# A new stored order, and a new split between VectorE and ScalarE, for a fused attention and MoE kernel

## The chip, the cores and the metric

The kernel runs on one core of a Trainium2 chip. The time is that of the device, in microseconds (us): three runs of the kernel before gave 565.9, 566.43 and 566.93, median 566.43. The profile is of one execution, and its span, from the first to the last instruction, is 563.2 us.

## The reference

Two stages. The first is a linear attention with a complex decay, for 4 batches and 8 heads of 768 positions and 48 dimensions. The second is a feed-forward layer over the 3072 rows that the first one leaves.

```python
scale = np.minimum(mag, 0.999) / (mag + 1e-06)      # mag = |a|
for t in range(S):
    S_re, S_im = ar * S_re - ai * S_im + k[t] v[t]^T, ar * S_im + ai * S_re
    y[:, :, t] = q[:, :, t] @ S_re
h = x @ w_in                                        # x: 3072 x 384, w_in: 384 x 2048
out = (h * sigmoid(1.702 * h)) @ w_out              # w_out: 2048 x 384
```

## The kernel before

The 768 positions of a batch are three units of 256, so there are 12 units (u = 0 to 11), each of two chunks of 128. A unit goes through three stages.

*prepare* turns the decay into running products (scans over time) and multiplies them into q and k. Unit 0 does it in two parts of 128 positions, so that its first chunk can start early. The lines that count here: L393, L409 and L427 are scans, L401 and L402 a reciprocal of 3 columns, L437 and L440 belong to the angle, and L271 is the product (`qr` and `qk` are q and k with the factors in). POOL copies three columns (L458), then SP issues five DMAs for each of the two tensors (L469 to L472) that spread the heads over the partitions of `qkh`.

*attend* works on `qkh` with small matmuls on quarters of the array. A group is one entry of the plan: P (L507, scores into `p_ps`, 32 profiled matmuls), T (L563, two transposes of k into `kz_ps`), X (L532, output into `x_ps`, 8 to 32 matmuls) and Z (L557, the new state into `kz_ps`, 32 matmuls). Between them VectorE masks the scores (L511, `pm`), and ScalarE or VectorE copies the transposes (L566 or L567, `kt`) and the result (L542 or L543).

*moe* is the feed-forward layer, in blocks of one unit (blocks 0 and 1) or two units (blocks 2 to 6). Blocks 0 and 1 use float32 weights `valA` and `valU`. The later ones split every number into two fp32r halves and take three matmuls for a product, of 128x512. L613 is the first product (into `h_ps`) and L646 the second (into `o_ps`). Between them come the activation (L626, ScalarE), the high half (`gh`, a cast: L629 on ScalarE or L630 on VectorE) and the low half (`gl`, L632, VectorE).

The weights arrive as 64-bit words in four buffers `raw`. ScalarE takes one half (L294), VectorE the other (L291, then a shift L295), and L298 adds them into `valA` or `valU`. A buffer can be loaded again when its sum is done. Later the float32 weights are split in two (L307 or L308, and L310). In the rest of the run, 58 looks at the inputs (`raw_w`, L675 to L699) test whether this fast path holds.

The order of all this is not found at run time. Each of the 1,827 operations is an entry of a plan, with an engine, a function and the entries it depends on. A table `ORDER` holds the sequence in which they are written into the program, and that fixes the sequence on each engine; an engine takes its own instructions in that sequence and waits at each for what it needs. The set `OTHER` lists those of 282 entries with two forms, one for ScalarE and one for VectorE, that take the second form. When an entry needs a ScalarE function table other than the current one, a table load (L843) is put ahead of it.

Before the first attention there are 13 entries (L454, 26 profiled matmuls) that only keep TensorE busy until real work is there; the result is not used.

Of the kernel before, what the change touches and what calls it, by code (L numbers as in the profile page):

```python
# [106 lines left out]
}  # L107
ORDER = (
    "08jve0000A00jUK0A&DD08s!_0D}O808{{l0962n09F8p09OEr09gP509XKB0E++v0Eqw#09pWF09yc$00sbz0FVG&0A2u!0AT=)0AK)-0Am1-"
    "0Ac|U0FwZ}00#hQ0I2|y0G9w{0BHaM0BQgX0A~PZ0Bitj0F(f20Ga^^0B!*Z0F?l50SW+{0B``70C50w0TBS40GR-u0CE8m0G$930CWJK0D%CQ"  # L110
    "0H6R30CfQq0CoVP0Tcjt0HFY*0C)fr01*JB0HpyH00aQC0T}?Q0Hy&J0H*+X0Sf@L0JH!I0D1uz0H^?~0JQ)K0T=+b0IUHT022Uv0IdMH0DJ)-"
    "02u&%03!f?0Ji}k01g1I02BbP0J#8v0k#1f0Vn{v03HCq0J{O00I&eO0KovU0Vx2z0Kx#i0LTEt0K@>v0UZFv0V)8-0UiMi0UQ7%0LlQz0Du7@"
    "03`s_0VM#-0NMa10V4q`0U`hz0M!5|0M-B-02Kf?0N?-|02Tox0N4QB0k{Cy0L%a#0W1K{0NDT+0k;4x03QI)0O9}`0NVf{03iS<0WJX00Ve?A"
    "0MP+003rb105|~S05SmG0l5I*0VV;u0WbjP0lNV&0WkpN0lxvf0WtvQ0W$%;0L=lw05bsX04V{!04@M30PFxO05t&80W<*a0ObHI0W|>V0Sy5*"
    "051SK0O|ng05AYK0mA_605JgX05k!`0P+FB05$<Q0mcEs0S*B306YQ20Mh}-06_po0Pq3M0m%Um0YL#d0YU*o0Pz7j0Ym}M0XG4r0Y?Bk0XqQo"
    "0X+f8080Tp0Yw4J0QdpQ0Z0M<0Zjo(0Qmqt0Y(5m0nh<H0ZIWs06zfq0Qvy?06+mw0iXd(073!M0agG<0QLb_0Z#x!07L;$07wB$07U^<0YCuv"
    "0a*Y^0hRzv0RI8e07?K&0Z{<{0RaF`0n`D^0n-5d0nGvc0o4Hg0sjHk0RRC~0s#S20oMW80a^f00aOA40ipq10s{d80bK!A0t5mG0bT)O0ha;>"
    "0onoy0cipU0oeiD0b>FV0o(y!0uKRb0tEqO0v7=T0crvY0dE2f0;U050b~LV0t*5d0uTXo0R#aB0c!zn0R{pR0ucff0uuq>0bl{>0rUaj0cHW-"
    "0vQ1Z0cQcS0viEg0qFv#0ki>Z0jdFU0vZCX0pS650;mD%0pbC50vrOV0v!St0c`<r0;&Ps0dfKB0hs}$0eS+f0v`dI0u=#s0w4mg0v-YG0qg>?"
    "0;~cd0rdgz0ek`D0ptR-0p$Vk0rmlV0h|Hx0wV!<0eu3p0qp`L0<{7n0p<aQ0<!^k0h<Ay0wn?R0jvVJ0rvu~0f7OX0=fZt0p|j*0rLT{0fzyf"  # L120
    "0=5Bw0=WYF0=EJ90e%7|0j>hS0=xl(0x$w60r>*J0x<#l0=ohG0x|+T0sH}f0fGX-0{j7l0sR8Q0w@AA0{sDn0>lFX0jL5g0f_;K0yF|D0yY9G"
    "0yhFZ0{#Ll0xbcd0yqLL0gVFx0zLvY0yzRd0xtoh0y+Xl0?z{g0g3{?0y_f*0=)r?0|o-e0gM7i0zd(e0>}c!0!RWu0|5fb0geJf0!acx0>T1H"
    "0z?8#0>uH40!0E#0|NsG0#gFZ0i^>30|^3B0#^dc0}2BO0?Y#q0?h(V0g(d_0!{&v0$l=F0}cZV0#pJ|0#ySH0h0rm0$c)F0h9t(0$~Fb0$KwR"
    "0$u@?0jC2M0?-2x0#E|k0$Ty80$&3b0%ihY0$>7B0?q<t0%!vh0~i8h1DXR80%rpm0@?!61DOLC0~-Qm0&4@C0~!My0%-%B0^0&?0&xQ!0^9>0"
    "0jmOP1DyhG0@MQ110VyU0^I?v0^b861ET_N0^kFr0^S3j1Em6R1EvDg1E&KY0&fGV0&)W)0(AqR0j~n#1FQn(1D^ub0^$PJ0&@c60_6hN0`CK%"
    "0(%1R1E>Pn1E~V>1FiwF0(t^=10(|E0(1iB0(b)Q0(=5@1F-`20_XyL1F{110_g(k0)GLs0_y_y0_*{`10@1}273bc1FHgs1MCAP0{8>70__5M"
    "27Cjw0`vp011AE20{H_d11<uD27LoB27Uti1FZsr0)YeV1Fr+M0)qqY0)_*(27dyF0*M1K0*(TT12G1G1GWN)27v?f13Cha1Gxf=1G)l?27&^U"
# [890 lines left out]
```

## Time and profile before

| | |
|---|---|
| median of 3 runs | 566.43 us (565.9 to 566.93) |
| span of the profiled execution | 563.2 us |
| TensorE (PE) busy | 532.4 us, 95% |
| VectorE (DVE) busy | 447.3 us, 79% |
| ScalarE (ACT) busy | 313.2 us, 56% |
| first matmul | at 24.61 us |
| first matmul of the feed-forward layer | at 43.63 us |
| first matmul of block 2 (128x512) | at 154.22 us |
| last matmul | at 558.94 us |

The profile gives busy time by engine, in total and for any stretch, what every engine waited for, and the instructions in order of time. The own time of the profiled execution is not listed; its span is 3.2 us under the median of the runs, so about that much lies around the span. A busy TensorE is not one at its peak: matmuls overlap, so the distance from start to start counts, not the duration. For a 128x512 matmul in a row of its kind this distance is 0.227 us, while the row shows 0.39.

### The profile page before, as it was taken

How to read it: one execution, taken by the hardware profiler on the slowest of the kernel's cores; microseconds unless marked ns; L12 is line 12 of the kernel's file. 1: busy time of each engine (PE TensorE's matmuls, PEld its weight loads, DVE VectorE, ACT ScalarE, POOL GpSimd, SP SyncE). 2: the span in 40 equal slices, each digit the busy share in tenths (PEclk: the TensorE clock that was granted, in tenths of full speed). 3: DMA queues.
4: the chain of work that ended last, by engine and by line, in shares of the span. 5: the costliest groups of instructions: out<-in, count | busy, mean ns of one | idle time of the engine just before them, and what ended most of it. 6: DMA issues, size and time to landing. Idle time of an engine off the chain costs nothing.

```text
span 563.2 us, 14767 instructions
## 1 busy us (share of the span) xinstructions
PE 532.4 (95%) x6236; PEld 442.2 (79%) x6236; DVE 447.3 (79%) x820; ACT 313.2 (56%) x460; POOL 24.5 (4%) x86
## 2 busy tenths in 40 slices
PE   0289999999999999999999999999999999999997
PEld 0268888888888888888888888888888888888885
...
GB/s 307 199 194 359 181 381 76 222 102 221 72 146 119 128 148 101 113 150 122 136 180 75 167 128 210 45 227 94 103 138 56 203 122 87 51 52 70 29 61 110
DMA packets 30902, 80.06 MB, mean 142 GB/s; under 512 B 4208, under 2 KB 7024, under 8 KB 30832
## 3 DMA queue, kind: packets, MB, share of 16 engines
...
q14 instruction: 21, 0.17, 0.1%
HBM read 55.44 MB, written 4.72 MB: 107 GB/s over the span
## 4 chain that ended last, share of the span: by engine, by line
PE 92%; DVE 5%; ACT 1%; DMA 1%; issue 0%; DVEq 0%
PE o_ps L646 37%; PE h_ps L613 37%; PE x_ps L532 7%; PE p_ps L507 5%; PE kz_ps L563 4%; PE kz_ps L557 3%; DVE s L427 1%; DVE qk L271 1%; DMA ri<-in_a_dram 1%; DVE pm L511 1%; DVE s L271 0%; DVE qr L271 0%; DVE s L409 0%; DVE s L393 0%; DVE valA L298 0%
## 5 line engine op out<-in xcount | busy, mean ns | idle before, releaser
L626 ACT ACTIVATE g<-h_ps 128x512 f32<-128x512 f32 x80 | 46.3, 596 | 120.8 <-PE h_ps L613 79.7
L613 PE MATMUL h_ps<-xhi,hiA 128*128 128x512 f32 x240 | 95.9, 400 | 0.0
L646 PE MATMUL o_ps<-gh,hiU 128*128 128x512 f32 x240 | 95.5, 398 | 0.0
L646 PE MATMUL o_ps<-gl,hiU 128*128 128x512 f32 x240 | 93.7, 390 | 0.0
L613 PE MATMUL h_ps<-xhi,loA 128*128 128x512 f32 x240 | 93.6, 390 | 0.0
L646 PE MATMUL o_ps<-gh,loU 128*128 128x512 f32 x240 | 93.5, 390 | 0.0
L613 PE MATMUL h_ps<-xlo,hiA 128*128 128x512 f32 x240 | 93.5, 389 | 0.0
L843 ACT ACT_TABLE_LOAD x61 | 78.3, 1283 | 1.9 <-PEq L1006 0.8
L630 DVE CAST gh<-g 128x512 fp32r<-128x512 f32 x70 | 29.4, 421 | 42.5 <-PE o_ps L646 25.5
L632 DVE TENSOR_TENSOR gl<-g,gh 128x512 fp32r<-128x512 f32 x80 | 54.5, 684 | 3.0 <-ACT gh L629 1.3
L646 PEld LDWEIGHTS o_ps<-gl,hiU 128*128 128x128 f32 x240 | 45.0, 188 | 10.0 <-DVE gl L632 0.4
L613 PEld LDWEIGHTS h_ps<-xhi,loA 128*128 128x128 f32 x240 | 45.0, 188 | 9.6
L680 DVE TENSOR_REDUCE fit<-raw_w 128x1 f32<-128x256 f32 x96 | 38.1, 413 | 18.0 <-DMA raw_w<-in_w_out_dram 17.7
L646 PEld LDWEIGHTS o_ps<-gh,hiU 128*128 128x128 f32 x240 | 45.1, 188 | 9.2 <-issue 0.4
L646 PEld LDWEIGHTS o_ps<-gh,loU 128*128 128x128 f32 x240 | 45.1, 188 | 8.7
L613 PEld LDWEIGHTS h_ps<-xlo,hiA 128*128 128x128 f32 x240 | 45.1, 188 | 8.5
L613 PEld LDWEIGHTS h_ps<-xhi,hiA 128*128 128x128 f32 x240 | 45.1, 188 | 8.5
L511 DVE TENSOR_TENSOR pm<-p_ps,mask 128x512 f32<-128x512 f32 x48 | 32.8, 682 | 17.2 <-PE p_ps L507 13.9
L566 ACT ACTIVATE kt<-kz_ps 128x224 f32<-128x224 f32 x66 | 23.3, 353 | 40.5 <-PE kz_ps L563 29.9
L271 DVE TENSOR_TENSOR qk<-qk,s 128x768 f32<-128x768 f32 (+1 forms) x52 | 45.7, 889 | 0.0
L646 PE MATMUL o_ps<-g,valU 128*128 128x256 f32 x192 | 45.3, 380 | 0.0
L613 PE MATMUL h_ps<-x,valA 128*128 128x256 f32 x192 | 45.0, 381 | 0.0
...
## 6 DMA issues: line engine op xcount, KB each, us to landing
...
```

Source lines behind the costliest of these rows:

```text
L271: add(en, t, rank, lambda: e.tensor_tensor(out=out, in0=a, in1=b, op=alu), **kw)
L507: mm(p_ps[to : to + QL, j, lo:L], lhsT=at(h, 1, c)[:, lo : lo + QL], rhs=at(h, 0, c)[:, lo:L], start=True, stop=True)
L511: add("DVE", d_t(CW), rk(4 * c + hh), lambda hh=hh: dve.tensor_tensor(out=pm[hh], in0=p_ps, in1=mask, op=ALU.mult), r=["P"], w=[f"pm{hh}"])
L532: mm(x_ps[32 * j : 32 * j + 32, r, :], lhsT=lt, rhs=rt, start=n == 0, stop=n == len(steps) - 1)
L566: one = ("ACT", a_t(2 * KD) - 0.12, lambda e=e: act(out=kt[0][:, 2 * e : 2 * e + 2, :], in_=k_ps, func=AF.Copy))
L613: mm(h_ps[hb][:, hs], lhsT=ww[:, r * T + f * P : r * T + (f + 1) * P], rhs=x[:, r, :], start=r + k == 0, stop=r == NR - 1 and k == len(ter ...
L626: add("ACT", a_t(N) - 0.15, rk(i + f / 2), lambda hb=hb, hs=hs: act(out=g32[hb][:, hs], in_=h_ps[hb][:, hs], func=AF.Silu, scale=SLOPE), r ...
L630: two = ("DVE", d_t(N, 2), lambda hb=hb, hs=hs: dve.tensor_copy(out=high.g(hb)[:, hs], in_=g32[hb][:, hs]))
L632: add("DVE", d_t(N), rk(i + f / 2), lambda hb=hb, hs=hs: dve.tensor_tensor(out=glo[hb][:, hs], in0=g32[hb][:, hs], in1=high.g(hb)[:, hs].b ...
L646: mm(o_ps[m][:, 0:N], lhsT=y[:, f * DM + m * P : f * DM + (m + 1) * P], rhs=x[:, hs], start=i == 0 and f == 0 and k == 0, stop=i == NP - 1 ...
L680: add("DVE", d_t(CK), rk + 2, lambda x=x, op=op: dve.tensor_reduce(out=f_w[:, x, n : n + 1], in_=weights.looked_at()[:, :, 1], op=op, axis ...
L843: nc.scalar.preload_act_table_set(o[5])
```

## The change

Two tables are replaced: `ORDER`, the sequence, and `OTHER`, the entries in their second form. No operation is added or taken away, and the functions are the same. (Two more lines in `OTHER` move every line number behind it by 2, so L613 of before is L615 of after.)

```diff
 OTHER = {
-    260, 261, 262, 349, 351, 412, 418, 420, 426, 432, 434, 436, 440, 449, 489, 491, 497, 511, 512, 522,
...
+    262, 341, 402, 403, 404, 424, 426, 428, 440, 449, 511, 512, 580, 597, 600, 607, 610, 620, 630, 637,
...
 ORDER = (
-    "08jve0000A00jUK0A&DD08s!_0D}O808{{l0962n09F8p09OEr09gP509XKB0E++v0Eqw#09pWF09yc$00sbz0FVG&0A2u!0AT=)0AK)-0Am1-"
...
+    "08jve0000F0A&D|00jWQ0I2{`015z70E7Tj08{{j0962m09gQ50EPeo09pWD0EYkr0A2uF0Ehrr09*hN0E+-&0EqyK0FMA;0E_@)0FVHY0F3}-09"
...
```

`OTHER` grows from 51 entries to 113. Entries for VectorE fall from 718 to 662, and those for ScalarE rise from 399 to 455. The largest part is the cast `gh`: 38 more of them are ScalarE's and 5 more VectorE's. Table loads rise from 61 to 66.

On VectorE, in the head of the program, this stood behind the second part of unit 0 and around its last products (`qr`, `qk`), up to the first mask of scores (`raw_71` to `raw_74` are the four weight buffers):

```order
L291 TENSOR_SCALAR valA_238<-raw_74 128x768
L271 TENSOR_TENSOR qk<-qk,s_84 128x3x128
L295 TENSOR_SCALAR raw_73<-raw_73 128x768
L271 TENSOR_TENSOR s_82<-s_82,s_81 128x3x256
L271 TENSOR_TENSOR qr<-qk,s_80 128x3x128 x2
L295 TENSOR_SCALAR raw_74<-raw_74 128x768
L271 TENSOR_TENSOR qk<-qk,s_85 128x3x128
L298 ISA valA_154<-raw_71,valA_154 128x1536
L271 TENSOR_TENSOR qk<-qk,s_85 128x3x128
L370 SCALAR_TENSOR_TENSOR s_81<-ri,s_82 128x3x256
L295 TENSOR_SCALAR raw_72<-raw_72 128x768
L511 TENSOR_TENSOR pm_95<-p_ps,mask 128x512
```

The two shifts among the products (L295 of `raw_73` and `raw_74`) now stand behind them. In the same place there is now:

```order
L293 TENSOR_SCALAR valU_229<-raw_73 128x768
L293 TENSOR_SCALAR valA_233<-raw_72 128x768
L273 TENSOR_TENSOR qk<-qk,s_83 128x3x128
L442 TENSOR_SCALAR small<-s_85 128x3
L300 ISA valA_154<-raw_71,valA_154 128x1536
L273 TENSOR_TENSOR s_82<-s_82,s_81 128x3x256
L273 TENSOR_TENSOR qk<-qk,s_84 128x3x128
L273 TENSOR_TENSOR qr<-qk,s_80 128x3x128 x2
L273 TENSOR_TENSOR qk<-qk,s_85 128x3x128 x2
L372 SCALAR_TENSOR_TENSOR s_81<-ri,s_82 128x3x256
L513 TENSOR_TENSOR pm_95<-p_ps,mask 128x512
```

The shifts L297 (L295 of before) of `raw_74` and `raw_73` come between this mask and the next one.

On TensorE, a typical short burst of attention between feed-forward matmuls (here within block 3) was P followed by T:

```order
L613 MATMUL h_ps_106<-xhi_2082,loA_1187 128x512
L507 MATMUL p_ps<-qkh_76 32x128 x4
L507 MATMUL p_ps<-qkh_76 32x96 x4
L507 MATMUL p_ps<-qkh_76 32x64 x4
L507 MATMUL p_ps<-qkh_76 32x32 x4
L563 MATMUL kz_ps<-ident,qkh_76 128x112 x2
L646 MATMUL o_ps_107<-gh_1749,hiU_1196 128x512
```

In the order of after it is T that comes first (again within block 3):

```order
L615 MATMUL h_ps_106<-xhi_2174,loA_1272 128x512
L565 MATMUL kz_ps<-ident,qkh_76 128x112 x2
L509 MATMUL p_ps<-qkh_76 32x128 x4
L509 MATMUL p_ps<-qkh_76 32x96 x4
L509 MATMUL p_ps<-qkh_76 32x64 x4
L509 MATMUL p_ps<-qkh_76 32x32 x4
L648 MATMUL o_ps_107<-gh_1765,hiU_747 128x512
```

From the first feed-forward matmul on there were 64 such bursts, 33 of them begun by T and 56 ended by T. There are now 66, of which 63 begin with T and 29 end with it.

## Rows read from the trace of the kernel before

**Rows 1.** What PE waited for: total us, times, longest; the largest.
```profile
PE h_ps L454 <- DVE small L440: 24.6, 1, 24.6
```

**Rows 2.** Busy time by stretch: stretch, length, then PE, PEld, DVE, ACT, POOL.
```profile
24.60:43.60 19.00, 17.00 (x326) 12.99 (x326) 18.68 (x30) 15.19 (x24) 2.30 (x6) 1.00 0.61 193
43.60:154.20 110.60, 110.60 (x1509) 95.02 (x1509) 106.56 (x175) 93.62 (x140) 6.51 (x20) 1.00 0.67 199
```

**Rows 3.** PE in order of time, first feed-forward group: start, us, operation.
```profile
43.63 5.43 PE L613 MATMUL h_ps<-x,valA 128*128 128x256 f32 x24
```

**Rows 4.** PE in order of time, the last two matmuls.
```profile
558.94 0.19 PE L716 MATMUL p_ps<-small 128*1 128x1 f32 x2
```

**Rows 5.** DVE in order of time, within 24 to 42 us.
```profile
24.50 0.55 DVE L291 TENSOR_SCALAR valA<-raw 128x768 int32<-128x768 int32 x1
24.97 0.55 DVE L271 TENSOR_TENSOR qk<-qk,s 128x384 f32<-128x384 f32 x1
25.44 0.55 DVE L295 TENSOR_SCALAR raw<-raw 128x768 int32<-128x768 int32 x1
25.91 0.95 DVE L271 TENSOR_TENSOR s<-s,s 128x768 f32<-128x768 f32 x1
...
28.78 0.95 DVE L298 CUSTOM_DVE_ANT_0 valA<-raw,valA 128x1536 uint16<-128x1536 uint16 x1
29.64 0.55 DVE L271 TENSOR_TENSOR qk<-qk,s 128x384 f32<-128x384 f32 x1
...
30.98 1.01 DVE L295 TENSOR_SCALAR raw<-raw 128x768 int32<-128x768 int32 x1
...
40.74 0.69 DVE L511 TENSOR_TENSOR pm<-p_ps,mask 128x512 f32<-128x512 f32 x1 [0.25 <-PE p_ps L507]
41.35 0.68 DVE L383 TENSOR_SCALAR s<-s 128x768 f32<-128x768 f32 x1
41.95 0.94 DVE L437 SCALAR_TENSOR_TENSOR s<-s,s 128x768 f32<-128x768 f32 x1
```

**Rows 6.** Line L401: count, duration ns shortest/median/longest, first and last start.
```profile
L401 DVE TENSOR_SCALAR small<-s x13: 143/160/1140, 13.1 to 421.1; 128x3 f32<-128x3 f32 x13
```

**Rows 7.** POOL in order of time, two stretches of the head.
```profile
13.22 0.98 POOL L721 MEMSET qkh<- 128x513 f32 x2
...
30.26 0.85 POOL L458 COPY qk<-fit 128x3 f32<-128x3 f32 x1 [1.82 <-DVE qk L271]
```

**Rows 8.** SP's queue in order of time, last DMAs of unit 0.
```profile
33.58 1.24 SPq L472 DMA_DIRECT2D qkh<-qk  x2
```

**Rows 9.** PE in order of time: around a burst X P Z T.
```profile
361.60 0.39 PE L613 MATMUL h_ps<-xhi,loA 128*128 128x512 f32 x1
361.92 0.43 PE L532 MATMUL x_ps<-pm,v 128*32 128x128 f32 x8
...
363.89 0.39 PE L613 MATMUL h_ps<-xlo,hiA 128*128 128x512 f32 x1
```

**Rows 10.** PE in order of time: around a burst T P X Z.
```profile
483.37 0.40 PE L646 MATMUL o_ps<-gl,hiU 128*128 128x512 f32 x1
...
485.70 0.40 PE L646 MATMUL o_ps<-gh,loU 128*128 128x512 f32 x1
```

**Rows 11.** PE in order of time: P of two bursts Z P T.
```profile
298.48 0.99 PE L507 MATMUL p_ps<-qkh 128*32 128x128 f32 x32
...
383.61 0.73 PE L507 MATMUL p_ps<-qkh 128*32 128x128 f32 x32
```

**Rows 12.** ACT over the whole run by line, the cast on ACT.
```profile
L629 ACT ACTIVATE gh<-g 128x512 fp32r<-128x512 f32 x10 | 6.3, 628 | 12.1 <-PE o_ps L646 12.0
```

**Rows 13.** ACT from 43.6 to 154.2 us by line: busy us, mean ns | idle before.
```profile
L843 ACT ACT_TABLE_LOAD x16 | 20.5, 1283 | 0.3
...
L566 ACT ACTIVATE kt<-kz_ps 128x224 f32<-128x224 f32 x14 | 5.0, 356 | 2.0 <-PE kz_ps L563 2.0
...
L307 ACT ACTIVATE hiA<-valA 128x768 fp32r<-128x768 f32 x4 | 3.5, 872 | 0.0
```

More of the change, by code (lines that the diff above doesn't have):

```diff
@@ L124 @@
[L124 to L127, printed above, removed]
-    "0`3Fv10w_Q0+|E21Mvg91NH;*12h9E12O|D12Y3V12qHp11kcM12zLJ0*wQ_0+9nZ0+Ivt0+<6W13U(U0+a@X12_Y{0-6Iq1Hc140+j-m13m-#"
@@ new lines @@
+    "Js4l0Ji|S0Vn{v0J{Jl0K5UV0KEYk0KfnU02Khp0UH2+0Kou&0LcLy022TQ0Kx#i03!gg0Vx2(0VM#$00{uf0L1{y02Tno0V)6)0XP860U-d#0Mq"
+    "~%0V4p_03QI>0V@F_03ZM%0L}p003-ky03`t60VDt@0M`MQ0N4Sz044#q0NDX20M7v304D(A0W1LF02%-{0WAO`0NMZ>02}}^0l5J#0PFzc0386_"
+    "0MG#@0NwyC0Wbl&0N(*G0Wkr)0Sf^P0OSBT0Wtx<0Sy5&0S*8;0OkNG0S^Gt06G9F0W<*T04o7C05bsX0X6_G0O$ZT06PHX0PX-V051S60Qdmu0l"
+    "Wa}06YLO0lfh005t$X0lopl0l)yw0P_LG0l@$^0P+FC0mK2v07d}t0mcE#0nP#b0m%T;080Tm0Pg`!0Q3Pt0Qmtz0Mh{a0XhMi06hTl0QCXL06qX"
+    "e0Yd>d0XqRi06+oH0X+dl073xv0XzUh07L<p0QUh#07U>t0Y?D-0Z0ML0Z9P=0ZIV?0nh;Z07wB=07(Hp0n!1?0Y3rL07?N)0ZReR0i*!@0p0*i0"
@@ new lines @@
+    "ssL|0Q~_#0oDNl0apM`0ayXm0oMUg0a*e60Zakd0bBvm0Z{=`0n`Cn08Rl@0bKx30aOA30bT(D0aXG50onm#0s{fr0owuy0RsXA0o(!!0jvRI0tN"
+    "yM0tEsM0tW$T0R#dH0cinS0t*5T0b~JX0bc<H0d4}O0jdE80uTXa0uKRa0ucfd0kQ%U0u%uU0p9^&0c!#m0dE1c0rUZC0;d6W0bv3d0pJ1X0dWD{"
+    "0pS5~0ipsK0c-*30vZAv0pbDb0u=#m0vrMs0;mCW0v-Y#0qX)E0eS&<0d@kZ0w4k*0e}J{0;&O*0we))0;>Wd0<Zz@0;~b!0j2@$0rdhU0<i+L0p"
+    "tOh0p$Vj0<{9J0<r;f0p<bi0<!_00=NNq0<Qt~0eJ$t0=5By0ek`Q0<8h}0h<AV0{a5D0=WU80>1%!0j>dl0=xn70p|hu0fqs60=oh*0f+(e0>A<"
+    "%0ww|T0x<#k0>J^C0r~;^0fPaZ0>c4+0>S~G0z3l60sI0e0gM9u0igoK0=@z=0x1Ig0=)r*0y6>q0{#Jo0xAOk0yYB10xJSN0{{ZY0yF|F0|f#t0"
@@ new lines @@
+    "|5fa0gVF50yhFK0zLx+0yqN80fz!P0|o;L0?Yz60!9M|0xtqT0iyys0|)~O0g3`g0y_dg0?GnN0zm<Z0!acw0}TSr0geJg0!jiz0!#x00}la<0!s"
+    "r60gwVk0}KNK0#XAM1DFAi0!;z10!{-C0g(Zy0#pH|0#yQ20}%rd0~G?#0#5;w0h0n;0jC020$2g51DOLB0$l=G1DXM=0h9vS0hIz_0~Z3&0#*YU"
+    "0#E_10$Kwa0j~oY0}=vW0$T#w0#O2A0}}%r0%ihY1DgXK0~-UJ0^0&$10Dir0kH#}10VyU0%QVX10eyk0%!rX0%Zbg1D*zZ1EvF@0&oIp10MsS0?"
+    "`8^0&D_t0?q>51ET_J1E>R}1D^ul1Em9}0@4EA0@DMj0&WBB0^kB|1F-^f0^tI027Cju27Ll^0(Aqk1Fiyk0(J&|0^$PR0(1ka0`CHR0@MQ40^<V"
+    "a1FHk90`LOl0@eeq0(b)?0_6gC1GNLR0_OsI1GfXP0(}GX1GWP30)7I20)zwZ27d;C1MLI327v<C0(k@P1G)m(0`dd!1Fr)00_X$10`mfe0_g(w1"
@@ new lines @@
+    "HJ?C27&_g1NH;B0`~@k0_p<z1H1-=1NQ>!0_+3w1NZ{@0)PX*10@3b1M~wU0)hkj1N8!d1N#H{289BH28IJB0*M3s0)_^M0*3?s0*?fh0__7j1OE"
+    "g71N{Py0*V5Q0*C|x1O)@T11<w611|$G0*nL(0+R#>0+0fY11JQS0`3Db28aX!12h9N11SS411kcQ1eOMg0+9xa13LpX0+j>_0+<6l1PTNQ0+Iv^"
+    "1egMu0-6IX11$st0+s@u12YDT28;v*28{%n12zLa0-FOj13v_s13m*d0-OSu1fK*91Pub90-ggo295-v1e*e%1Ih%Q13(6k1Hl9l29N}v13?531f"
+    "c{H0-*y!1f>L`1QP>81e^q>14IMD1fv9`1g8T<14aU(14jmt1gQiL15O5#14#s^29pA#14snk1Iq%W1J(qt155)@1gir|29yI>29*S=29^X515X1"
+    ">15pI815yLb15*RT1h4~I15E_q1mFa+1mOg;16Br?2ABg>2AKm@1Hc6016c&)1mpu(1g!&I16u=P16%~?2AT$&1hE5N2Al-!17HHB1I+`(17rlW1"
@@ L151 @@
+    "N4Dq1|0?$1$_n>1|9`|1%L+<1{ntv1%Cz~1|S9@1%U=41|tR}1%d`81||k41}FwD1}O$F1~3JK1}X+C1~>;41~UbO1%(DI2Neb_1~CRQ208{d1~d"
+    "jW2Nnkx1~&#f20RBC1~~^A20{is20jKr21Eu-21N!&2O0)H2O9=M22KV+2OI`R2OS1h21o`;22BP^21^D{22ciA22=)722uu723H1I23iJS23rPU"
+    "24V(P25JUe23-ba23`hV24e<f25bgs24)6l25Saw25tsv25$y%25|;-266^>2Ob7`2OkD=26YB_2OtJ^26+b|2O<"
 )
```

53 lines of the change are left out of this document (17 added, 36 removed), and 7 rows, old and new, of the table OTHER.

## Prediction

> **What bounds the kernel now.** I read TensorE's waits first, then its busy time by stretch, and last the order of time around the places that wait. TensorE stands idle for the first 24.6 us, which is one wait, the only long one it has [rows 1]. From 24.60 to 43.60 it is busy for 17.00 of 19.00 us, but part of that is the group that only keeps it warm. From 43.60 to 154.20 it is busy for all of 110.60 [rows 2]. So behind the first feed-forward matmul, at 43.63 [rows 3], TensorE is the bound, and no other engine holds it up. Only three things can move the end: when that matmul starts, how long TensorE's own stream takes from there to 558.94 (515.3 us), and a new wait in it. Behind the last matmul [rows 4] come 4 us for the last evacuation and store; they keep their form in the new order, and I leave them as they are.
>
> In the head it is VectorE that sets the pace: 18.68 us busy of 19.00 [rows 2]. It makes q and k for both chunks of unit 0, masks their scores, and the last of these masks, at 40.74 [rows 5], releases the last X group, whose result the first feed-forward matmul reads.
>
> **The head, by VectorE's queue.** Steps below are from start to start, which is what a step takes in the queue.
>
> Two shifts L295, 0.47 each (25.44 to 25.91), stood ahead of the last product of unit 0 and now stand behind it: -0.94. L401 usually takes 0.16 us and once 1.14, at 13.1 [rows 6], while POOL ran two memsets of 0.98 together at 13.22 [rows 7]. In the new order these memsets stand behind the two copies that POOL makes from the finished products, so L401 meets none of them: -0.98. From there to the last mask the two shifts come back (+0.94). One more half-word L291 stands there (24.50 to 24.97, +0.47) and one clamp L383 of the next unit (41.35 to 41.95, +0.60), while one sum L298 has moved behind the mask (28.78 to 29.64, -0.86). The 0.25 us that VectorE waited for the scores at 40.74 goes, because the products are earlier: -0.25. All of it in [rows 5]. The sum is -1.92 + 1.15 - 0.25 = -1.02. I take -1.0.
>
> The bounds are -2.4 and 0. The lower one is all that comes off ahead of the products, with nothing given back, and some 0.4 for smaller gaps. The upper one is SP: it issues the twenty DMAs for the heads of unit 0 in a row, the last two from 33.58 on for 1.24 us [rows 8]. The new order needs its last product before the second ten can start and has the same twenty to issue, so their landing is no earlier. If the last scores wait for that landing, nothing is gained. The last mask stands 6 us behind it, so I take VectorE's queue.
>
> By the Trainium skill, "SBUF — State Buffer", section "Who interferes with whom", a VectorE tensor_scalar of the two-port kind and a GpSimd operation lock each other out, and whichever starts first keeps the ports to its end. The trace agrees with 1.14 us where 0.16 is usual, beside the memsets. The rule speaks against this gain, because a memset that is moved can meet another tensor_scalar; the sum would then be about 1 us less.
>
> **TensorE's stream behind 43.63.** The groups are the same, but one Z group of unit 0 is now ahead of the first feed-forward matmul and is work off the stream; I cost it at 0.45 us, from the two bursts below (they differ in order alone, and Z takes less than a fifth of 2.3): -0.45.
>
> What changes most is how bursts of attention open and close. With the order X P Z T, the time from the last big matmul before the burst to the second one behind it is 363.89 - 361.60 = 2.29 us [rows 9]. With T P X Z, the same groups, it is 485.70 - 483.37 = 2.33 [rows 10]. T at the front is cheap to enter, but what follows it and the way back to big matmuls cost as much again. So a burst that is turned costs +0.04. By the order, 63 bursts begin with T instead of 33, and 29 end with it instead of 56: 28 turned, +1.1 us. The two further bursts I leave out; they are within this estimate.
>
> P directly behind a Z is uneven: in a burst Z P T at 298.48 it takes 0.99, in one at 383.61 0.73 [rows 11]. Five bursts of before have this form, and three of them show the long P; one burst of the new order has it. Four fewer at an average of 3/5 x 0.26 = 0.16: -0.65. Bounds: 0, if the long P returns in other forms, and -0.8 if all three go.
>
> Stream: -0.45 + 1.1 - 0.65 = 0.0, with bounds of -2.5 (below, rival 1) and +1.1.
>
> **The split of VectorE and ScalarE.** A cast `gh` takes 0.63 us on ScalarE [rows 12], and 38 more are now there. Nearly all of them stand behind 154 us, where a group of nine big matmuls takes 9 x 0.227 = 2.04 us, longer than activation, cast and low half each, so these are covered. The place to look at is from 43.63 to the first matmul of block 2, before at 154.22. By the order ScalarE gets two more table loads in it (2 x 1.283), six more copies `kt` (6 x 0.356) and four more conversions L307 (4 x 0.872) [rows 13], 8.2 us, and the other differences add about 0.4 at the same means. So 93.62 becomes about 102 of 110. VectorE loses seven copies and five casts, gains three products L271 of 0.95 and one set of scans, and comes out about 1.2 us higher: 106.56 becomes 107.8. In the head it ran at 18.68 of 19.00, 98%, and 107.8 of 110.2 is 98% too, so I cost it at 0. If it doesn't hold, the price is that of rival 2, and the bounds are 0 and +3.1.
>
> **Sum.** -1.0 (head) + 0.0 (stream) + 0 (split) = -1.0, on a span of 563.2. This span is 3.2 us under the median, and I take the same distance for after: 566.4 - 1.0 = 565.4.
>
> **Rival 1, the turned bursts pay.** A T at the front would save what a P pays on entry, without giving it back on leaving. Entering with P, X or Z costs about 0.09 us more than with T: in [rows 9] the last big matmul starts 0.32 before the first small one instead of 0.227 (361.60 to the burst at 361.92). 28 turned bursts give -2.5 instead of +1.1. With the Z group, the uneven P and the head at -1.0 that is -4.6: 561.8. For it speaks that the entry is visibly cheaper; against it, that 2.33 is not under 2.29. Chance 0.17.
>
> **Rival 2, ScalarE becomes late (slower).** Place: between 43.63 and block 2. ScalarE was idle there for 110.6 - 93.62 = 17.0 us, mostly waiting for results of TensorE and VectorE, and would now have 110.2 - 102 = 8.2 us for that, with VectorE at 98% beside it. It decides as soon as ScalarE's unavoidable waits in that stretch pass 8.2 us: what is over comes out as a wait of TensorE. If two thirds of the 17.0 stay, 11.3, that is 3.1 us too many: 565.4 + 3.1 = 568.5. For it: two engines near full that wait for each other. Against it: waits of an engine that runs ahead vanish when it has more to do, and in the head VectorE held 98%. Chance 0.20.
>
> **Rival 3, the memsets meet another shift.** POOL's memsets now come when the masks and shifts of the head are in VectorE's queue. One L295 at 30.98 took 1.01 instead of 0.55 [rows 5], beside POOL's copy of 0.85 at 30.26 [rows 7]. If two do that, 0.9 us comes back: 566.3. Chance 0.13. This is the rule of the Trainium skill named above ("SBUF — State Buffer", "Who interferes with whom") at work.
>
> **How the numbers follow.** About 0.2%, 1.1 us, is what a measurement of this kernel can tell from no change. The forecast, 565.4, has the remaining chance of 0.50; its own range is 564.3 to 566.4. It lies close to the line at 565.3, so I give 0.24 of it to faster and 0.26 to the same. Rival 1 is faster (0.17). Rival 2 is slower, but for a part of 0.03 in which its price is eaten by the gain. Rival 3 counts 0.10 for the same and 0.03 for slower. That makes 0.41 faster, 0.39 the same and 0.20 slower. The range for 8 in 10 goes from 561.8, rival 1 at its price, to 568.5, rival 2 at its price.
>
> **What would show it.** The first feed-forward matmul (L615) should start at about 42.6; at 43.6 the head gave nothing, at 41.3 all. L403, the reciprocal's clamp, should show no 1.14. From there to the last matmul the distance should be 515.3 again, within 1; over 516.5 with a wait of TensorE's weight loads for `g`, `kt` or `pm` is rival 2, and under 513.5 with none is rival 1. The bursts should keep the two sums, 2.29 and 2.33. The prediction is wrong if the distance shrinks by over 2 us, if TensorE stands still anywhere behind 44 us, or if the head moves by over 2.4.

## The result: 1.2% slower, and the profile after

Four runs of the changed kernel gave 572.14 to 573.8 us, median 572.58; four of the kernel before, 565.41 to 566.93, median 566.16. The ratio is 1.0117, with an interval of 1.0103 to 1.0132. The forecast was 565.4, within 561.8 to 568.5. The time rose instead of falling, and it lies 4.1 us above the upper end.

The profiled execution took 572.14 us, with a span of 570.4 where before had 563.2: +7.2. (What lies around the span is about 1.7 us in nearly every run here; I had put 3.2 around it, so on the span I was wrong by 8.2.) I read the changes from the start of the first feed-forward matmul of each block; "block 0" is the stretch from its first such matmul to that of block 1. The views are those of [rows 2 to 4]: busy time by stretch (start and end, length, then PE, PEld, DVE, ACT, POOL, granted clock, DMA share, GB/s), before and after.

```profile
43.63:95.42 51.79, 51.79 (x624) 44.51 (x623) 50.88 (x85) 46.84 (x70) 4.04 (x11) 1.00 0.79 255
95.42:154.22 58.80, 58.80 (x889) 50.51 (x887) 55.67 (x92) 46.77 (x71) 2.47 (x9) 1.00 0.57 149
```

```profile
44.62:98.65 54.03, 52.14 (x597) 44.35 (x592) 51.41 (x81) 46.12 (x69) 4.87 (x13) 1.00 0.81 242
98.65:159.83 61.18, 59.85 (x888) 51.00 (x886) 57.14 (x91) 55.93 (x82) 2.68 (x14) 1.00 0.60 145
159.83:247.55 87.72, 87.71 (x1092) 72.73 (x1091) 84.17 (x142) 70.22 (x99) 2.13 (x11) 1.00 0.56 143
247.55:565.89 318.34, 318.16 (x3313) 262.98 (x3311) 191.17 (x370) 142.55 (x212) 3.71 (x20) 1.00 0.41 106
```

| us | before | after | |
|---|---|---|---|
| first feed-forward matmul at | 43.63 | 44.62 | +0.99 |
| block 0 | 51.79 | 54.03 | +2.24 |
| block 1 | 58.80 | 61.18 | +2.38 |
| blocks 2 to 6, to the last matmul | 404.72 | 406.00 | +1.28 |
| behind the last matmul | 4.26 | 4.57 | +0.31 |

Two thirds of the loss are in blocks 0 and 1. TensorE, which before was busy for all of their 110.59 us, stands still there. These are its largest waits, in order of time (in brackets the wait and what ended it):

```profile
53.50 4.15 PE L615 MATMUL h_ps<-x,valA 128*128 128x256 f32 x18 [0.63 <-ACT g L624]
58.12 4.15 PE L648 MATMUL o_ps<-g,valU 128*128 128x256 f32 x18 [0.28 <-ACT g L624]
77.12 1.56 PE L615 MATMUL h_ps<-x,valA 128*128 128x256 f32 x6 [0.33 <-ACT g L624]
94.52 0.41 PE L565 MATMUL kz_ps<-ident,qkh 112*128 112x112 f32 x2 [0.50 <-DVE st L574]
110.86 2.86 PE L615 MATMUL h_ps<-x,valA 128*128 128x256 f32 x12 [0.65 <-ACT g L624]
120.66 1.56 PE L615 MATMUL h_ps<-x,valA 128*128 128x256 f32 x6 [0.47 <-ACT g L624]
151.87 0.41 PE L565 MATMUL kz_ps<-ident,qkh 112*128 112x112 f32 x2 [0.20 <-DVE st L578]
```

They sum to 3.06. From start to start a wait costs more than its row says: around the first, the 9 matmuls ahead of it and the 18 behind take 6.73, where 27 of them usually take 5.84, so 0.9 is lost instead of 0.63. TensorE lost 5.07 in the two blocks: 2.24 + 2.38 and the 0.45 of the Z group that block 0 no longer has. In the reckoning from start to start these waits come to about 5.0, together with two smaller ones that only the weight loads show (0.3 at 67.33 for a `g`, 0.5 at 92.91 for a `kt`). So waits account for both blocks.

**The first wait has its cause on VectorE.** First DVE, then POOL, then ACT in order of time:

```profile
45.94 2.77 DVE L297 TENSOR_SCALAR raw<-raw 128x768 int32<-128x768 int32 x1
48.63 0.54 DVE L293 TENSOR_SCALAR valA<-raw 128x768 int32<-128x768 int32 x1
```

```profile
45.91 2.39 POOL L723 MEMSET qkh<- 128x513 f32 x5
```

```profile
49.21 1.08 ACT L296 ACTIVATE valA<-raw 128x768 uint16<-128x768 uint32 x1 [1.64 <-DVE valA L293]
```

A shift of 0.55 us took 2.77: it started 0.03 us behind the first of five memsets and ended 0.4 us behind the last. ScalarE then waited 1.64 us for the next clamp, and the activation behind it was late for TensorE at 53.5.

**Others come from the place in ScalarE's queue.** ACT ahead of the wait at 110.86:

```profile
106.25 1.28 ACT L845 ACT_TABLE_LOAD   x1
107.54 0.85 ACT L390 ACTIVATE s<-s 128x768 f32<-128x768 f32 x1
108.29 0.83 ACT L309 ACTIVATE hiU<-valU 128x768 fp32r<-128x768 f32 x1
109.12 1.28 ACT L845 ACT_TABLE_LOAD   x1
110.42 0.38 ACT L624 ACTIVATE g<-h_ps 128x256 f32<-128x256 f32 x1
```

The input of this `g` was ready at about 105.3, when ScalarE took up the `g` of the group ahead of it. It stands behind two table loads of 1.28, which bring in one preparation step and go back, and behind a conversion. (In the profiles, table loads in the whole kernel went from 61 to 62 and not to 66; ahead of block 2 there are two more, 18 instead of 16, as the prediction reckons.) The wait at 77.12 has the same form. Those at 58.12 and 120.66 are of another: two feed-forward groups that write halves of one PSUM bank follow each other, and the activation of the first half starts only when the second group has ended.

```profile
120.23 0.38 ACT L624 ACTIVATE g<-h_ps 128x256 f32<-128x256 f32 x1 [1.16 <-PE h_ps L615]
```

Whether the program's own semaphores ask for that or something else does isn't shown.

**The head** answers to [rows 3, 5, 6, 8], by DVE, PEld, SP and PE, each in order of time:

```profile
38.54 0.69 DVE L513 TENSOR_TENSOR pm<-p_ps,mask 128x512 f32<-128x512 f32 x1 [0.61 <-PE p_ps L509]
...
40.55 0.68 DVE L513 TENSOR_TENSOR pm<-p_ps,mask 128x512 f32<-128x512 f32 x1
```

```profile
37.71 0.63 PEld L509 LDWEIGHTS p_ps<-qkh 128*32 128x32 f32 x26 [0.42 <-DMA qkh<-qr]
```

```profile
35.61 1.23 SPq L474 DMA_DIRECT2D qkh<-qr  x2
```

```profile
42.81 0.43 PE L559 MATMUL kz_ps<-v,kt 128*32 128x48 f32 x20
...
44.34 0.35 PE L559 MATMUL kz_ps<-v,kt 128*16 128x48 f32 x12 [1.09 <-issue]
44.62 2.86 PE L615 MATMUL h_ps<-x,valA 128*128 128x256 f32 x12
...
565.83 0.19 PE L718 MATMUL p_ps<-small 128*1 128x1 f32 x2
```

VectorE's queue was ahead as reckoned up to the third of the four masks: the first came at 29.54 instead of 31.91 and the second at 31.84 instead of 34.27. The third could have started at about 37.8, behind the clamp, 1.0 earlier than before. It waited 0.61 us for its scores, whose matmuls waited for the last remap DMA to land, and came at 38.54 instead of 38.85; the last came at 40.55 instead of 40.74. SP issued the last pair of remap DMAs at 35.61, 2.0 us later than before: the second ten of them begin at 29.56 instead of 28.46, and one pair among them takes 2.15 where the longest of before takes 1.17. Then the Z group that now stands ahead of the first feed-forward matmul waits 1.09 us in its middle, for nothing that another engine does ("issue").

### The profile page after: what moved, and what is told of

It reads as the page before. It is cut to its first block, busy times and chain, and to the rows that moved or that the text cites. A ratio compares the mean times of both kernels' runs of the same rounds, so it can differ in the third digit from the quotient of the medians.

```text
span 570.4 us, 14760 instructions
## 1 busy us (share of the span) xinstructions
PE 535.9 (94%) x6236; PEld 444.9 (78%) x6236; DVE 424.1 (74%) x764; ACT 353.2 (62%) x517; POOL 22.7 (4%) x86
## 4 chain that ended last, share of the span: by engine, by line
PE 71%; DVE 2%; issue 0%; ACT 0%; DVEq 0%
PE o_ps L648 30%; PE h_ps L615 28%; PE x_ps L534 5%; PE p_ps L509 3%; PE kz_ps L565 2%; PE kz_ps L559 2%; DVE gl L634 0%; DVE qk L273 0%; DVE qr L273 0%; DVE pm L513 0%; DVE s L439 0%; DVE s L372 0%; DVE s L257 0%; DVE gh L632 0%; DVE s L437 0%
## 5 line engine op out<-in xcount | busy, mean ns | idle before, releaser
L615 PE MATMUL h_ps<-xhi,hiA 128*128 128x512 f32 x240 | 96.1, 400 | 0.0
L615 PE MATMUL h_ps<-xhi,loA 128*128 128x512 f32 x240 | 93.7, 390 | 0.0
L615 PE MATMUL h_ps<-xlo,hiA 128*128 128x512 f32 x240 | 93.6, 390 | 0.0
L615 PEld LDWEIGHTS h_ps<-xhi,hiA 128*128 128x128 f32 x240 | 45.0, 188 | 9.8 <-issue 0.6
L615 PEld LDWEIGHTS h_ps<-xhi,loA 128*128 128x128 f32 x240 | 45.1, 188 | 9.6
L615 PEld LDWEIGHTS h_ps<-xlo,hiA 128*128 128x128 f32 x240 | 45.1, 188 | 8.6
L682 DVE TENSOR_REDUCE fit<-raw_w 128x1 f32<-128x256 f32 x96 | 36.5, 412 | 19.1 <-DMA raw_w<-in_w_out_dram 15.5
L631 ACT ACTIVATE gh<-g 128x512 fp32r<-128x512 f32 x43 | 26.9, 628 | 35.9 <-PE o_ps L648 35.6
L615 PE MATMUL h_ps<-x,valA 128*128 128x256 f32 x192 | 45.4, 384 | 2.1 <-ACT g L624 2.1
L615 PEld LDWEIGHTS h_ps<-x,valA 128*128 128x128 f32 x192 | 35.5, 190 | 8.2 <-ACT g L624 3.5
```

Of the source, the lines that this page charges most:

```text
L615: mm(h_ps[hb][:, hs], lhsT=ww[:, r * T + f * P : r * T + (f + 1) * P], rhs=x[:, r, :], start=r + k == 0, stop=r == NR - 1 and k == len(ter ...
L631: one = ("ACT", a_t(N) - 0.1, lambda hb=hb, hs=hs: act(out=high.g(hb)[:, hs], in_=g32[hb][:, hs], func=AF.Copy))
L682: add("DVE", d_t(CK), rk + 2, lambda x=x, op=op: dve.tensor_reduce(out=f_w[:, x, n : n + 1], in_=weights.looked_at()[:, :, 1], op=op, axis ...
```

## The experiments

A plan entry has a number; an edit moves it behind another one in the list `order`. Each ratio is against runs of the kernel before on the same chip.

**The memsets, from both sides.** In the first kernel the memsets of after go where none of these shifts is; in the second, those of before go to where after has them.

```diff
 # e1_memsets_early: after
+        for n in (271, 270, 269, 268, 267):
+            order.remove(n)
+            order.insert(order.index(266) + 1, n)
```


> The changed kernel with one edit: the five memsets L723 that POOL runs in a row at 45.91 us stand behind the memset at 31.55 instead, where VectorE has products, a packed conversion and scans. Theory A (the five memsets hold VectorE's shift L297 for 2.77 us instead of 0.55, and the 5.0 us in which TensorE stands still in blocks 0 and 1 are mostly this delay handed on): L297 at about 46 takes 0.55, TensorE's standstill in blocks 0 and 1 falls from 5.0 to at most 2.8, the time from 572.6 to between 567.6 and 570.4. Theory B (ScalarE has 8 us more work there and is late whatever VectorE does): L297 takes 0.55, but the standstill stays above 4 us and the time within 0.7 of 572.6.

```diff
 # e4_memsets_late: before
+        for n in (271, 270, 269, 268, 267):
+            order.remove(n)
+            order.insert(order.index(305) + 1, n)
```


> The kernel before, with one edit: five of its eight memsets L721 stand in a row behind POOL's copy at 45.72 us, as in the changed kernel. Theory A: VectorE's clamp L291 at 47.18 or its shift L295 at 47.65 is held until the memsets end, 1.0 to 2.3 us, TensorE stands still behind it, and the time goes from 566.2 to 567.2 to 568.5. Theory B (ScalarE's load decides): VectorE may be held, but TensorE makes it good, and the time stays within 0.4 of 566.2.

Before with late memsets: ratio 1.0026 [1.0016, 1.0036], and block 0 grew from 51.79 to 52.89. POOL, DVE and PE's wait:

```profile
45.40 2.80 POOL L724 MEMSET qkh<- 128x513 f32 x5
```

```profile
45.44 2.29 DVE L294 TENSOR_SCALAR valA<-raw 128x768 int32<-128x768 int32 x1
```

```profile
PE o_ps L649 <- ACT g L625: 0.7, 1, 0.7
```

So the mechanism is real and costs about 1.1 us in block 0. (Here the shift was held over four of the five memsets; the fifth then took 0.94 instead of 0.53.) But after with early memsets was 571.35, ratio 1.0107 [1.0084, 1.013]. The shift took 0.54 and VectorE was 1.86 us earlier, yet block 0 stayed at 54.04: VectorE then waited for a transfer of weights. The gain in time came ahead of block 0, where the "issue" wait was 0.18 and the first feed-forward matmul came 0.95 earlier, at 43.67. That the memsets are most of the loss is refuted.

```profile
65.19 0.56 DVE L296 TENSOR_SCALAR valA<-raw 128x768 int32<-128x768 int32 x1 [2.62 <-DMA raw<-in_w_in_dram]
```

**The Z group**, moved back behind the first feed-forward matmul (entry 204 behind 213), alone and together with the memsets.

> The changed kernel with one edit: the Z group that stands directly ahead of the first feed-forward matmul stands behind the first twelve of them. Theory F (TensorE ran out of instructions in this Z: many short matmuls before the 16 KB of instructions asked for at 42.03 us were usable): the 1.1 us wait on 'issue' at L559 goes, the first feed-forward matmul starts at about 42.9 instead of 44.62, and with 0.4 us of Z now in the stream the time falls by 1.3, from 572.6 to about 571.3. Rival G (the wait belongs to what this Z reads): it moves with Z, the first feed-forward matmul starts at about 42.9, a wait of about 1 us stands at L559 behind it, and the time stays within 0.4 of 572.6.

> The changed kernel with both edits, the five memsets early and the Z group behind the first twelve feed-forward matmuls. Theories A and F together: the two gains add up, 566.3 to 569.1. Theory A alone: as the run with the memsets alone, within 0.4. Theory B and rival G: within 0.7 of 572.6. If VectorE is the limit from the head on, the earlier start is lost again and this run is equal to that with the memsets alone.

The "issue" wait went, and the first feed-forward matmul then waited 0.64 us for ScalarE's copy of the attention result: start 43.66, block 0 54.21, 572.44, ratio 1.0128 [1.0107, 1.0149]. With both edits it was 571.77, 1.0113 [1.0084, 1.0142], and 53.75 for block 0. In this order Z fills a gap, so moving it back gains nothing that can be told.

**ScalarE's amount of work or its order.** One kernel gives 15 of ScalarE's entries in blocks 0 and 1 back to VectorE; the other leaves the amounts and moves two `g` and one `kt` ahead of the table loads that they stood behind (with the two edits above).

```diff
 # e6_act_engine: after
-        for n in OTHER:
+        for n in OTHER ^ {349, 351, 412, 418, 420, 434, 436, 489, 491, 497, 567, 569, 704, 765, 775}:
 # e5_act_order: after, e3_both and
+        239 behind 233, 363 behind 357, 343 behind 331
```


> The changed kernel with the order kept and fifteen instructions of blocks 0 and 1 given back from ScalarE to VectorE, as they were before (seven copies kt, five conversions L309, three of the rotation's preparation): 9.1 us less on ScalarE, some 7 more on VectorE. Theory B (the amount of ScalarE's work): TensorE's standstill in blocks 0 and 1 falls from 5.1 us to under 2, the time from 572.6 to 569.5 or less. Theory C (place in the queue): the waits at 76 and 110 us stay, the standstill stays at 4 or more, the time is 571.5 or more, and more than 572.6 if VectorE, busy for 95% of block 0, cannot take them.

> The changed kernel with the two edits of e3_both and three instructions moved forward in ScalarE's queue, no work changed: the activation g of H0.4 stands directly behind that of H0.3 instead of behind two table loads and four other instructions, the activation g of H1.1 directly behind the second one of H1.0 instead of behind two table loads, and a copy kt ahead of five instructions that TensorE does not wait for. Theory C (what costs is where g and kt stand in ScalarE's queue): the waits of TensorE at 76, 109 and 91 us, 0.58, 0.82 and 0.39, go, its standstill in blocks 0 and 1 falls from 4.2 (e3_both) to 2.4 to 2.8, and the time by 1.5 from that of e3_both, to about 570.2. Theory B (the amount of ScalarE's work): the waits come back elsewhere, the standstill stays above 3.8 and the time within 0.5 of e3_both, 571.8.

Less on ScalarE was worse: 576.05, ratio 1.0174 [1.0156, 1.0192]. Blocks 0 and 1 by stretch:

```profile
45.79:100.53 54.74, 52.07 (x591) 44.25 (x591) 52.38 (x85) 45.91 (x66) 5.04 (x13) 1.00 0.78 235
100.53:164.81 64.28, 60.82 (x887) 51.12 (x887) 62.91 (x104) 50.05 (x70) 2.53 (x14) 1.00 0.58 138
```

In block 1 VectorE is busy for 62.91 of 64.28, and TensorE loses 3.5 us. So with this order VectorE is the tighter engine in block 1. That ScalarE's amount is the cause isn't borne out, but no kernel here takes work off ScalarE without loading VectorE, so the amount alone isn't tested. The other kernel gave 571.35, 1.0088 [1.0074, 1.0101]: the waits at 77 and 111 were gone and block 1 fell to 60.46, but the one at 94 grew to 0.88 and a transfer of weights came 3.75 us late for VectorE.

**Taking the named waits away.** The pairs that share a bank are put apart, alone and with everything above but the Z group.

```diff
 # e10_bank_pairs: after
+        218 behind 217, 220 behind 225, 370 behind 372, 374 behind 370
 # e9_repaired: e10_bank_pairs, memsets early, 239 behind 233, 363 behind 357, 343 behind 331
```


> The changed kernel with nothing but the two feed-forward groups moved (H0.1 ahead of H0.2, O1.2 between H1.3 and H1.4) and their two activations with them. Theory C: the activation of H1.3 starts at the end of its own group and not of the next one, the waits of 0.53 at 57.6 and 0.74 at 119.8 go, 572.6 becomes 571.3. Theory E: the standstill in blocks 0 and 1 stays at 5 and the time within 0.5 of 572.6.

> The changed kernel, no work and no engine changed, with what theory C and theory A name put right together: the five memsets behind the one at 31.55 us, the three instructions forward in ScalarE's queue as in e5_act_order, and two feed-forward groups no longer directly followed by another one that writes the same half of PSUM (H0.1 goes ahead of H0.2, O1.2 goes between H1.3 and H1.4, each with its activation directly behind). Theory C (single instructions that stand too late or too close): of the 5.1 us in which TensorE stands still in blocks 0 and 1 the waits at 52.5, 57.6, 76.5, 110 and 119.8 go (0.9, 0.53, 0.58, 0.82, 0.74), 1.0 to 2.0 us are left for the chains of T and kt, or up to 3.3 if a weight transfer is late again at about 66 us, and the time goes from 572.6 to 568.5 to 570.0. Theory E (the new order asks for 8 us more of preparation ahead of block 2, and some wait must pay for it): the waits come back at other places, the standstill stays above 3.5, the time above 570.5.

Pairs alone: 572.67, 1.0121 [1.0107, 1.0136]. All together: 571.92, 1.0104 [1.0088, 1.012]. Each wait that was aimed at went, and others came. The larger waits of `e9_repaired` in blocks 0 and 1 up to Z of block 1:

```profile
68.94 1.56 PE L639 MATMUL h_ps<-x,valA 128*128 128x256 f32 x6 [1.09 <-ACT g L648]
95.83 0.41 PE L589 MATMUL kz_ps<-ident,qkh 112*128 112x112 f32 x2 [0.87 <-DVE st L598]
```

Block 0 was 54.02 again and block 1 60.42. That the loss can be taken away wait by wait is refuted.

**Which stretch of the order loses.** These kernels take one table up to a point and the other behind it (an entry keeps the engine of the table that it comes from).

```diff
+        first = first[:393]    # before's table up to block 1; 624: to block 2, 177: to block 0
+        order = list(first + tuple(n for n in order if n not in first))
```


> The order and the engines of before up to the first matmul of block 2, then what is left in the order and on the engines of after. Theories B and C (the loss is in blocks 0 and 1): TensorE does not stand still between 43.6 and 154 us, from there to the end it takes 404.7 as before plus 0.5 for waits of T behind a feed-forward group plus 0.6 for the turned bursts, and the time is 0.8 to 1.6 above that of before. Rival D (the 38 casts gh on ScalarE and the turned bursts behind block 2 cost most of it): the time is 4 or more above that of before.

> The order and the engines of before up to the first matmul of block 1, then what is left in the order and on the engines of after. At that point before has done 5.1 us of work on VectorE and ScalarE that after has not, and after 2.6 that before has not. If block 0 of the new order is where the time is lost: no standstill up to 95 us, in block 1 at most the 2.1 us that after has there, and a time of 566.2 + 2.1 + 1.1 = 569.4 or less. Theory E (the new order asks for more vector work ahead of block 2 than VectorE and ScalarE can do): what block 0 does not pay comes out in block 1, whose standstill rises to 4 or more, and the time is 571 or more.

> The order and the engines of before up to the first feed-forward matmul, then what is left in the order and on the engines of after. If the head's order (memsets, the Z group, the order in which conversions are done) causes the waits of block 0: the first feed-forward matmul starts at 43.6, the standstill in block 0 falls from 3.0 to under 1.5, the time to 569.5 or less. Theory E, or single waits of block 0's own order: the first feed-forward matmul starts at 43.6, block 0 keeps 2.5 us or more, and the time is 571.0 to 572.5.

> The order and the engines of after up to the first matmul of block 1, then what is left in the order and on the engines of before. If block 0 of the new order is where the time is lost, and the old order goes on from there without waits: standstill 3.0 in block 0 and under 0.7 behind it, 566.2 + 1.0 (head) + 3.0 = 570.2. Theory E: block 0 stays behind by 2.5 us of vector work that the old order then has to make good, so that block 1 stands still for 2 us or more as well, and the time is 572 or more.

| kernel | us | ratio | block 0 | block 1 |
|---|---|---|---|---|
| before's head, then after | 573.74 | 1.0157 [1.0143, 1.017] | 54.38 | 61.19 |
| before to block 1, then after | 569.65 | 1.0079 [1.0066, 1.0093] | 51.78 | 60.98 |
| before to block 2, then after | 572.33 | 1.0105 [1.009, 1.0121] | 110.58 with block 1 | |
| after to block 1, then before | 573.67 | 1.0138 [1.0123, 1.0154] | 54.36 | 63.51 |

The first two rows differ in the order of block 0 and in the engine of three entries there (a copy `x`, a `kt`, a conversion). Block 0 loses 2.6 us with after's, behind before's head too (54.38 against 51.78), so the head doesn't bring it. (The profiled executions are 5.5 us apart; 2.55 of that is the seam: in the first row the first feed-forward matmul comes at 46.17 instead of 43.62, behind a wait of 0.97 for a `kt`.) In the second, block 1 stays at 60.98, as in after: what block 0 doesn't lose there does not come out in block 1. The fourth says little on block 0, since before's order behind it stands still in block 1 (63.51), 2.82 us of it in one wait at the seam. The third shows what the loss in block 1 buys. TensorE has no wait up to block 2, and then one of 4.1 us:

```profile
154.90:248.33 93.43, 89.33 (x1093) 73.89 (x1092) 88.57 (x148) 73.66 (x101) 3.60 (x15) 0.98 0.56 140
```

```profile
161.44 0.41 PE L616 MATMUL kz_ps<-ident,qkh 112*128 112x112 f32 x2 [4.10 <-ACT kt L619]
```

At the first matmul of block 2, after has done 8.0 us of vector work that before does later (nearly all of it the preparation of unit 4) and before 1.8 us that after does later; by block 3 after is 32.9 us ahead. Its blocks 2 and 3 ask for this work; joined to before's blocks 0 and 1 they find it undone. So block 1 of after is longer, I conclude, because more is asked for within it (VectorE is busy for 57.14 us in it instead of 55.67, ScalarE for 55.93 instead of 46.77). That is argued from the third kernel; none leaves this work out.

**The pair of block 1 alone**, in the best of these (370 behind 372, 374 behind 370):

> e12_before_to_b1 with one feed-forward group moved: O1.2 goes between H1.3 and H1.4, with the activation of H1.3 directly behind it. In e10_bank_pairs the wait of 0.74 at 119.8 went and 0.77 came back in an X group at 138.8, when VectorE was behind. Theory: with VectorE and ScalarE 2.5 us further at the start of block 1 nothing comes back; the wait at 116.93 goes, no X group waits, block 1 takes 60.2 instead of 60.98. Rival: the wait comes back as in e10_bank_pairs and block 1 stays within 0.2 of 60.98.

569.21, 1.006 [1.0046, 1.0075]. The pair's wait went, an "issue" wait of 0.70 in that kernel became 1.08, and block 1 was 61.33 instead of 60.98. It comes back here too.

**The casts alone**: before with the 38 `gh` on ScalarE.

> The kernel before with its own order and nothing but the engine of 38 casts gh changed, from VectorE (0.42 each) to ScalarE (0.63 each), the same 38 as in the changed kernel. As the prediction costs them (covered by groups of nine large matmuls of 2.04 us): TensorE does not stand still behind 154 us and the time stays within 0.4 of before. Rival: ScalarE gets 24 us more behind 154 us, where it was busy for 185 of 405 us; a cast that stands behind a table load and a preparation there makes TensorE wait, 0.5 to 1 us at each of several places, and the time rises by 1 to 4.

565.78, 1.0013 [0.9998, 1.0028], and TensorE has no wait behind 154 us. The largest part of the new split costs nothing.

Its profiled execution shows one thing more: block 0 took 53.01 in it, though it has before's order and engines there. VectorE stood still for a transfer of weights, where the same instruction of before came at 61.17 without a wait:

```profile
62.93 1.03 DVE L294 TENSOR_SCALAR valU<-raw 128x768 int32<-128x768 int32 x2 [1.54 <-DMA raw<-in_w_out_dram]
```

So a transfer can be late in one execution without any change of the order, and cost 1.2 us of block 0. Single profiles that differ by about 1 us there prove little. What after's order loses is more than that: 53.75 to 54.80 in the profile of every kernel that has it, against 51.78 in five of before's and 52.89 and 53.01 in the other two.

**The late transfer.** In the kernel with early memsets, three products of unit 1 now stand behind the clamp that waited, and with them the ten DMAs that they release.

```diff
 # e17_spread_late: e1_memsets_early
+        for n in (310, 309, 308, 307, 306, 303):
+            order.remove(n)
+            order.insert(order.index(46) + 1, n)
```


> The kernel with the early memsets, in which three products of unit 1 on VectorE (one qr, two qk) now come behind the clamp of the last of four weight buffers, so that the ten DMAs that spread unit 1 over qkh start behind the landing of these weights and no longer beside it. In the kernel with the early memsets the load was issued at 55.9, the spread from 58.56 on, and the clamp waited until 65.14, 9.2 us after the issue. Theory X (the load is late because it shares the DMA engines with the spread): it lands 7.0 us or less after its issue (in the changed kernel it was 7.0, where the spread began later beside it), so the clamp runs by 63.0. Theory Y (it is late by itself): over 8.5 us again, the clamp at 64.5 or later. The spread comes some 5 us later in either case, so the first P of unit 1 and TensorE will wait for it, and no gain of time is expected: 571 to 575.

SP's load, ahead of the spread now (which begins at 64.66), and DVE's clamp:

```profile
57.37 0.33 SPq L297 DMA_DIRECT2D raw<-in_w_in_dram  x1
```

```profile
63.15 0.56 DVE L299 TENSOR_SCALAR valA<-raw 128x768 int32<-128x768 int32 x1 [1.31 <-DMA raw<-in_w_in_dram]
```

The load took 5.8 us from issue to landing instead of 9.2 beside the spread. That fits a load that was late because the two shared the DMA engines, in one execution of each. The time, 572.27 (1.0123 [1.0106, 1.014]), and block 0, 53.89, didn't move.

**After, run again unchanged**: 572.53, 1.0126 [1.011, 1.0142].

> The changed kernel once more, as it is. What belongs to the order comes back: L297 held for over 2 us beside five memsets, waits at about 57.6, 76.5, 92 to 94, 110, 119.8 and 151, blocks 0 and 1 together 4.5 to 5.5 us longer than before. What belongs to one execution may not: the wait on 'issue' of 1.1 us ahead of the first feed-forward matmul, and a late weight transfer at about 66 us. The time is 1.0103 to 1.0132 of before.

Each of the waits above came back within 0.05 us, the "issue" wait with 1.10 and the long shift with 2.78. They belong to the order.

**The memsets of before, out of the way.** The prediction costed the L401 of 1.14 us in before as worth 0.98. This kernel takes it away in the old order, and with it the hold of the shift L295 at 30.98 (1.01 instead of 0.55), beside which the last of the four memsets ran.

```diff
 # e7_before_memsets: before
+        for n in (267, 266, 265, 264):
+            order.remove(n)
+            order.insert(order.index(149) + 1, n)
```


> The kernel before, with the two memsets L721 at 13.22 us and the one at 31.05 moved behind POOL's copy at 15.47, beside scans, products and a fused multiply of VectorE. If VectorE's queue sets the head: L401 takes 0.16 instead of 1.14, L295 at about 30 takes 0.55 instead of 1.01, the first feed-forward matmul starts at 42.2 to 42.8 instead of 43.63, and the time falls by 0.8 to 1.4. If SP's row of DMAs for the heads sets it: L401 takes 0.16, the first feed-forward matmul stays within 0.3 of 43.63, the time within 0.3.

```profile
13.56 0.19 DVE L404 TENSOR_SCALAR small<-s 128x3 f32<-128x3 f32 x1
...
39.83 0.69 DVE L514 TENSOR_TENSOR pm<-p_ps,mask 128x512 f32<-128x512 f32 x1 [0.25 <-PE p_ps L510]
```

```profile
42.72 1.54 PE L616 MATMUL h_ps<-x,valA 128*128 128x256 f32 x6
```

It took 564.2 us, ratio 0.9964 [0.995, 0.9977], and beats both kernels. The last mask and the first feed-forward matmul came 0.91 earlier, and block 0 kept its 51.78. L401's part of that is about 0.45, since a wait for weights behind it grew by about 0.4; the shift's is 0.46.

## Why the prediction was wrong

**The step that failed** is "The split of VectorE and ScalarE … I cost it at 0". Its amounts came out as worked out: ScalarE 46.12 + 55.93 = 102.05 us (predicted 102), VectorE 51.41 + 57.14 = 108.55, of which 2.2 are the held shift (predicted 107.8). The conclusion from them was wrong. "107.8 of 110.2 is 98% too, so I cost it at 0" takes a busy share for a guarantee, but a share says nothing on which instruction is late. After's VectorE in block 0 is busy for only 51.41 of 54.03, less than 98%, and TensorE waits all the same, 5.07 us in blocks 0 and 1: for the `g`, `kt` and `st` that the order puts behind other work, or that come late through a buffer or a transfer.

**Rival 2** had the place and the direction right, and what would show it: over 516.5 from the first feed-forward matmul to the last (521.21), with weight loads that wait for `g` and `kt`. Its price was 3.1, the standstill 5.07. Its mechanism, ScalarE with too much to do, isn't borne out: `e6_act_engine` took work off ScalarE, and blocks 0 and 1 grew from 115.21 to 119.02 us, though VectorE got that work and so the amount alone stays untested. Shown instead: block 0 loses 2.6 us by its own table, the order with three changes of engine (the first kernel with two tables against the second), whatever the head ahead of it. Block 1 loses about as much, by the argument above because blocks 2 and 3 ask for work early.

**The head** was worth -1.0 by the sum and measured +0.99. Up to the third mask VectorE's queue behaved as reckoned: L403 has no row over 0.17 us any more (L401 before: 1.14), and `e7_before_memsets` shows that the two holds taken away in it are worth 0.91 on the path in the old order. The price of 0.98 went to L401 alone, where about half of the 0.91 belongs to it. But the last mask moved by only 0.19, so the upper bound, SP's row of remap DMAs, is what held: the third mask waited for scores, and these for the last remap DMA. I had taken VectorE's queue instead. Why SP's second ten come later and one pair of them slower is not shown; `qk`, the product of VectorE that they start from, now stands first in SP's sequence. The 1.09 us of the Z group's "issue" wait was no term at all.

**Rival 3** happened as a mechanism, and larger: I priced two shifts at 0.9 together, and one shift was held 2.2 us over its usual 0.55. The Trainium skill, "SBUF — State Buffer", section "Who interferes with whom", says the loser is blocked entirely; the trace agrees, and the price here is the whole row of five memsets rather than one of them. One reading behind the rival was wrong: the shift of 1.01 in before was held by the memset at 31.05, not by the copy of 0.85 ahead of it. In `e7_before_memsets` the same copy runs beside the shift, which then takes 0.55. In time the mechanism is worth about 1.1 us of block 0 in `e4_memsets_late` (+1.5 by the ratio), and in after nothing that can be told (`e1_memsets_early`).

**The stream** was right. Summed from the median step of each kind of group, without waits, it went from 512.9 to 513.5 us, +0.6, where the sum said 0.0 with a bound of +1.1: turned bursts +1.0, Z -0.45. The -0.65 for uneven P can't show in a sum of medians. In the traces it does: the three long P of before (298.48, 420.52 and 472.88, from start to start 0.92 instead of 0.66) are gone in after, about -0.8. Behind block 2 the other way weigh 21 turned bursts at +0.04, +0.8, and three bursts whose T stands behind a weight load that waits for `kt` or `st` (behind the big matmuls at 161.87, 349.64 and 371.17), +0.8. The rest of the +1.28 in blocks 2 to 6, some 0.5, isn't put down to anything; the windows above leave TensorE 0.2 us idle there. A T P X Z burst keeps its 2.33 of [rows 10]; the big matmuls around one of after:

```profile
236.87 0.40 PE L648 MATMUL o_ps<-gl,hiU 128*128 128x512 f32 x1
...
239.20 0.39 PE L648 MATMUL o_ps<-gh,loU 128*128 128x512 f32 x1
```

Rival 1, by which the turned bursts would pay, falls with that.

**Left open.** Why block 0 of after loses 2.6 us is not settled. Neither the memsets, nor the table loads, nor the bank pairs, nor the late transfer carries it: with each taken away it stays between 53.75 and 54.8, in one profile of each. One sign, and no more, is that in it the transfers are idle first and crowded later. The same stretches of before and of after (the DMA share is the last but one number):

```profile
48.00:56.00 8.00, 8.00 (x70) 6.75 (x70) 8.00 (x13) 7.64 (x15) 0.00 (x0) 1.00 0.89 322
62.00:66.00 4.00, 4.00 (x49) 3.25 (x48) 4.00 (x8) 3.97 (x6) 0.00 (x0) 1.00 0.73 131
```

```profile
48.00:56.00 8.00, 7.37 (x35) 6.17 (x34) 8.00 (x13) 6.66 (x11) 0.76 (x2) 1.00 0.60 207
62.00:66.00 4.00, 4.00 (x21) 3.51 (x20) 3.60 (x7) 3.97 (x7) 0.00 (x0) 1.00 1.11 214
```

After frees its four weight buffers one by one, so their loads go out at 50.07 to 57.77 instead of 47.29 to 55.04. An order that frees them earlier was not tried.
